# New numbers for the build-time ordering of a fused attention and feed-forward kernel

## The chip, the cores and the metric

The kernel runs on one core of one Trainium2 chip. Its time is the device time of one execution in microseconds; a kernel's time is the median of several runs. Beside it stands one execution taken with the profiler, whose engines, transfers and waits the profile shows. Engines are called TensorE (PE), VectorE (DVE), ScalarE (ACT), GpSimd (POOL) and SyncE (SP); SyncE only issues transfers.

## The reference

Causal attention with a decay bias over 8 batches, 8 heads, 576 positions and a head dimension of 64, then a feed-forward layer with an ELU over the 4608 tokens that result.

```python
scores = (1 / sqrt(D)) * q @ k^T                     # B=8, H=8, S=576, D=64
cum = cumsum(maximum(s, 0.0), axis=-1)
scores = where(causal, -1e9, scores + minimum(-(cum[:, :, :, None] - cum[:, :, None, :]), 0.0))
attn = softmax(scores);  out = attn @ v
x = out.transpose(0, 2, 1, 3).reshape(B * S, H * D)  # 4608 x 512
h = x @ w_in                                         # 512 x 2048
g = where(h > 0, h, exp(minimum(h, 0)) - 1)
return g @ w_out                                     # 2048 x 512
```

## The kernel before, in words

**Attention** goes by batch and by pair of heads. The queries of a batch are cut into blocks: 64 first rows (of both heads of a pair at once) and four blocks of 128. The blocks form pieces: first the lower two blocks of batches 0 to 3, then all four blocks of batches 4 to 7, then the upper two blocks of batches 0 to 3. The lower pieces of batches 0 to 2 are computed with float32 matmuls (the functions with low in their name); all others split each float32 operand into a high and a low float16 part, which VectorE, ScalarE and GpSimd prepare (prepare_pair). For each block TensorE makes the scores (L1065), VectorE adds the mask and keeps the row minimum of the negated scores (L1068), ScalarE takes the exponential and its sum (L1073), VectorE inverts the sum (L1078, L1079), and the scaled result is split into two float16 parts (the high one at L1125, L1127 or L1129, the low one at L1133, or at L1119 and L1120 on GpSimd). SyncE then turns these tiles with transposing transfers (turned_load, L409, tile T), and TensorE weighs the values with them (L1252). The result x goes to memory.

**The feed-forward part** takes 256 tokens at a time, 18 chunks. The first chunk is computed in float32 (native, L1423 and L1477); for it and for the low attention TensorE needs no split operands. For the others x (xh, xl) and the weights (wp) are split in high and low parts and three float16 products are added: first layer at L1427, then the ELU (L1439, L1446 or L1450, L1459, L1463, L1466), second layer at L1484. The weights come as 64-bit numbers (raws), are turned to float32 and split, at L697 to L717, in the first 160 us.

**The order.** All of this is described as operations of a class Plan. An operation has a priority, tiles that it reads and writes, and one or several ways: an engine, a cost in ns, and the instructions. Plan.issue orders them at build time. It keeps a clock of its own for each engine (free) and for the transfers (pipe). For every operation whose inputs are planned, it takes the earliest start: when the engine is free, when the inputs are ready (the end of the step that makes them plus a delay between the two engines, HOPS or HOP), when a buffer is free, and, for steps marked as users of the port that VectorE and GpSimd share (DVE-SB, Pool), not earlier than PORT_LEAD before the end of the last such step. The operation with the earliest start goes next, the lower priority number first where starts are equal; attention has lower numbers than feed-forward matmuls. Among its ways it takes the one with the least start plus cost, each cost multiplied by a bias of its engine: BIAS at first, STEADY_BIAS once the plan's TensorE is past STEADY_T (130 us of the plan). The bias serves the choice alone; the plan's clock takes the cost itself. A transfer takes its cost on SyncE and lands later by LAG, and not sooner than its bytes at RATE (bytes per ns) behind the transfer before. The order so found is fixed on every engine; at run time an engine waits wherever an input of its next instruction is late. SyncE's transfers stand in one queue in this order too.

In the first 60 us of the plan (FILL_T) a filler, a transpose of the identity (L1547), may go on TensorE where nothing else is planned to start within 350 ns (GAP).

The costs are the numbers in the calls of op, and the functions pe4 (a float32 matmul), pe16 (a float16 one), act_c and act_s, dve_p, dve_1, dve_2, pool_1 and pool_2, all of the number of columns n.

Of the kernel before, what the change touches and what calls it, by code (L numbers as in the profile page):

```python
# [34 lines left out]

LAG, RATE = 1800.0, 225.0
W0, WD = 25, 3
# [7 lines left out]
PRIO_LOW = 10  # L45
SP_COST, SP_SHORT, SP_TURN = 460.0, 600.0, 1320.0

# [49 lines left out]
class Plan:  # L97
# [9 lines left out]
    HOPS = {  # L107
        ("PE", "ACT"): 200.0, ("PE", "DVE"): 200.0, ("DVE", "PE"): 255.0, ("ACT", "PE"): 270.0,
        ("Pool", "PE"): 190.0, ("DVE", "ACT"): 130.0, ("DVE", "Pool"): 200.0,
        ("ACT", "DVE"): 140.0, ("ACT", "Pool"): 170.0, ("Pool", "DVE"): 75.0,  # L110
        ("Pool", "ACT"): 100.0, ("DVE", "DVE"): 75.0, ("PE", "PE"): 0.0, ("ACT", "ACT"): 75.0,
        ("Pool", "Pool"): 50.0,
    }
    HOP = 150.0

    BIAS = {"DVE": 1.3, "DVE-SB": 1.3}
    STEADY_BIAS, STEADY_T = {"DVE": 1.6, "DVE-SB": 1.6, "Pool": 1.5}, 130e3

    PORT_LEAD = {"DVE-SB": 240.0, "Pool": 120.0}

# [74 lines left out]
    def issue(self):  # L195
# [19 lines left out]
        while pending:  # L215
# [55 lines left out]
            self.log.append((engine, start, end, o.prio))  # L271
            free[engine] = end
            for b, k in o.new:
# [33 lines left out]
def pe(n):  # L307

    return max(0.4525 * n, 111.0)


def pe4(n):

    return 4 * pe(n)


def pe16(n):

    return n / 2.4 + 2.5

# [33 lines left out]

@with_exitstack
def kernel(
# [50 lines left out]
    def turned_load(prio, units, dst, src, reads, writes):  # L407

        op(prio, [("SP", SP_TURN, lambda: nc.sync.dma_start_transpose(dst(), src()), LAG,  # L409
                   units * P * P * 2)], reads, writes)  # L410

# [56 lines left out]
    def low_keys(tag):  # L468

        k = plan.buf(sb, [P, 2, LOW], F32, f"kl_{tag}", tag="st", bufs=N_ST)  # L470
        return k, [("Pool-M", pool_1(2 * LOW), lambda: pool.memset(k.v[HB:], 0.0))]

# [3 lines left out]
    def decay_sums():  # L476

        own = slice(HB, HB + 1)

        def row(m):  # L480
            return aux.v.rearrange("p m t -> p (m t)")[own, 2 * m * LOW : 2 * (m + 1) * LOW]

        load(-10, lambda: row(0).rearrange("p (h t) -> p h t", h=2), lambda: s[0:1, :2, :LOW],
             [], [(aux, "row")], 2 * LOW * 4)
        load(-9, lambda: aux.v[:NB, 0], lambda: s.rearrange("b h t -> (b h) t"), [], [(aux, 0)], NB * S * 4)
        op(-10, cleared, [], [(k_first, "sums")])

        def first():
            dve.tensor_scalar(row(0), row(0), 0.0, None, ALU.max)
            for h in range(2):  # L490
                sp, lo = (row(m)[:, h * LOW : (h + 1) * LOW] for m in range(2))
                dve.tensor_tensor_scan(lo, sp, sp, 0.0, ALU.add, ALU.max)
                dve.tensor_scalar(k_first.v[own, h], lo, lo[:, S // 2 : S // 2 + 1], 8.0,
                                  ALU.subtract, ALU.mult)
# [8 lines left out]
        for cost, step in (  # L503
            (460.0, lambda: dve.tensor_scalar(sp(), sp(), 0.0, None, ALU.max)),
            (1350.0, lambda: dve.tensor_tensor_scan(lo(), sp(), sp(), 0.0, ALU.add, ALU.max)),
            (590.0, lambda: dve.tensor_scalar(
                sp(), lo(), lo()[:, S // 2 : S // 2 + 1], 8.0, ALU.subtract, ALU.mult)),
        ):
            op(-9, [("DVE-SB", cost, step)], [], [(aux, 0), (aux, 1)])
        load(15, lambda: sums_dram.v, sp, [(aux, 0)], [sums_dram], NB * S * 4, lag=5000.0)  # L510
# [22 lines left out]
    def weigh(o):  # L533

        def rows():
            t = o.v[HB:, Q2].rearrange("p h t -> p (h t)")
            pool.memset(t, 0.0)
            for m in (2, 1, 0):
                pool.affine_select(
                    out=t, in_=t, compare_op=ALU.is_ge, fill=2.0 ** WEIGHT[m], base=-1 - m,  # L540
                    pattern=[[0, t.shape[1]]], channel_multiplier=1,
                )

        op(60, [("Pool-M", 5200.0, rows)], [], [(o, "weights")])
        op(60, [("Pool-M", 800.0, lambda: pool.memset(o.v[HB:, K2], 0.0))], [], [(o, "aux")])
# [27 lines left out]
    def zero_pad(prio, t, i):  # L573
        if pd[i] > pw[i]:
            op(prio, [("Pool-M", 70.0, lambda: pool.memset(t.v[:, pw[i] : pd[i]], 0.0))], [], [(t, "pad")])

# [60 lines left out]
    def scales_of(prio, spans, dst):  # L637
# [11 lines left out]
        def exponents():  # L649
# [6 lines left out]
        used = [(peaks, m) for at, k in spans for m in range(at, at + k)]  # L656
        op(prio, [("DVE-SB", 60.0 + 70 * n, largest)], used, [tops])
        op(prio, [("PE", pe4(P), lambda: pe_.matmul(flat.v[:, :P], tops.v, ident, start=True, stop=True))],
           [tops], [flat])
        op(prio, [("DVE", 600.0, exponents)], [flat], [own])  # L660
        op(prio, [("PE", pe4(P), lambda: pe_.matmul(every.v[:, :n], all_ones.v, own.v[:, :n], start=True, stop=True))],
# [4 lines left out]
    def weight_scales():  # L666

        scales_of(-600, [(A_IN, NF + 1), (A_OUT, NF + 1)], 0)
        op(-600, [("DVE-SB", 100.0, lambda: power(
            scales.v.bitcast(U32)[:, 3:4], scales.v.bitcast(U32)[:, 1:2], 2 * 127))],  # L670
# [92 lines left out]
    def prepare_low(u):  # L763
# [133 lines left out]
    def group_values(u):  # L897
# [8 lines left out]
        for j in range(NP):  # L906
# [35 lines left out]
    def prepare_pair(u, o):  # L942
# [111 lines left out]
    def softmax_block(prio, tag, native, pt, w, mask, mv, reads, operands, inv, view=lambda v: v):  # L1054
# [4 lines left out]
        for i in range(n):  # L1059
            sc = score_bank(f"sc_{tag}_{i}")  # L1060

            def scores(i=i, sc=sc):
# [3 lines left out]

            op(prio, [("PE", pe4(cw) if native else 2 * max(pe16(cw), 100.0), scores)], reads, [sc])
            op(prio, [("DVE", 84 + dve_p(cw), lambda i=i, sc=sc: dve.tensor_tensor_reduce(  # L1068
                pt.v[:, i * cw : (i + 1) * cw], sc.v[:, :cw], mv(i * cw, cw), scale,
                BIG if i == 0 else mn.v[:, 0:1], ALU.add, ALU.min, mn.v[:, i : i + 1]))],  # L1070
               [sc, mask], [(pt, "data"), mn])
        sm, col, last, ns, up = inv
        op(prio, [("ACT", 480 + w / 1.2, lambda: act.activation(  # L1073
            pt.v[:, :w], pt.v[:, :w], AF.Exp, bias=mn.v[:, n - 1 : n], scale=-1.0,
            accum_out=sm.v[:, col : col + 1]))], [mn], [(pt, "data"), (sm, col)])
        if last:
# [3 lines left out]

            op(prio, [("DVE-SB", 350.0, inverse)], [], [sm])

    def normalize(prio, pt, w, sm, col):
        r = slice(col, col + 1)
        op(prio, [
            ("Pool", 160 + 1.04 * w, lambda: pool.tensor_scalar(
                pt.v[:, :w], pt.v[:, :w], sm.v[:, r], 1.0, ALU.mult, ALU.mult)),
            ("DVE-SB", 220 + 0.7 * w, lambda: dve.tensor_scalar(
                pt.v[:, :w], pt.v[:, :w], sm.v[:, r], None, ALU.mult)),
# [4 lines left out]
    def halved(u, i, pt, sm, col):  # L1094
# [27 lines left out]
        for part, size, label in ((whole, k * P, "whole"), (rest, HB, "rest"))[: 1 + (i == u.last)]:  # L1122
            high, low = ((t16, (i, label, m)) for m in range(2))
            op(prio, [
                ("Pool", 160 + 1.04 * size, lambda part=part: pool.tensor_scalar(  # L1125
                    part(0), own(part), sm.v[:, r], 1.0, ALU.mult, ALU.mult)),
                ("DVE-SB", 220 + 0.7 * size, lambda part=part: dve.tensor_scalar(  # L1127
                    part(0), own(part), sm.v[:, r], None, ALU.mult)),
# [227 lines left out]
    def chunk_scales(ch, rows):  # L1356
# [8 lines left out]
        def steps():  # L1365
# [287 lines left out]
```

## Time and profile before

| what | us |
|---|---|
| median of 3 runs (1038.25 to 1038.91) | 1038.66 |
| the profiled execution's own time | 1034.6 |
| its span, first to last instruction | 1032.8 |
| its mean granted TensorE clock | 0.996 of full |

In the profile a matmul's end is modelled, so that a busy TensorE need not be at its peak, and groups of matmuls overlap each other: their busy times do not add up. An idle time stands with the instruction that ended it and with its releaser. L1427 is line 1427 of the kernel before; out<-in are tile names. The stretches that the prediction uses are these: 0 to 75 us, when weights and first inputs are loaded and TensorE also runs fillers; 75 to 150, the float32 chunk, with the weights being split; 150 to 920, attention and feed-forward together; from 920 to the end, feed-forward alone.

### The profile page before, as it was taken

Reading aid. Unit: us, or ns where it says so; the run is one execution under the profiler, and the core shown is the slowest. Engines: PE = TensorE matmul, PEld = TensorE weight load, DVE = VectorE, ACT = ScalarE, POOL = GpSimd, SP = SyncE. Lnnn points to the kernel's source line nnn. Section 1 sums busy time; section 2 is a strip of 40 time slices with the busy share of each in tenths; the row PEclk is TensorE's granted clock in tenths of the full one; section 3 lists DMA queues with packets and bytes.
Section 4 is the critical chain, followed back from the end, with each engine's and each line's share of the span. In section 5 each row is a group of like instructions: output and inputs, shape, how many; then the busy total and the mean of one; then the engine's idle time right before and its main releaser. Section 6 shows DMA issues by size and latency. Waiting matters only on the chain. (4 is left out here: it accounts for less than half of the span.)

```text
span 1032.8 us, 21782 instructions
## 1 busy us (share of the span) xinstructions
PE 1003.1 (97%) x7305; PEld 688.7 (67%) x7305; DVE 845.2 (82%) x2346; ACT 669.0 (65%) x1559; POOL 295.9 (29%) x487
## 2 busy tenths in 40 slices
PE   8889999999999999999999999999999999999998
PEld 6667656676666666666666666676666676666665
DVE  7999998788988988898889999798988898863232
ACT  4898755666667766776776766666675765644343
POOL 6343452242323323241234242222232123100000
PEclk9999999999999999999999999999999999999999
DMA  7997524589979997999989987979998998841000
GB/s 197 276 289 236 150 72 95 124 190 213 222 166 212 207 192 165 198 202 208 196 174 201 232 179 174 229 181 192 215 198 196 227 202 187 182 94 47 1 21 21
DMA packets 296724, 179.83 MB, mean 174 GB/s; under 512 B 209908, under 2 KB 270564, under 8 KB 296612
## 3 DMA queue, kind: packets, MB, share of 16 engines
q1 hardware_dynamic: 296612, 178.45, 75.7%
q8 instruction: 57, 0.93, 0.4%
q14 instruction: 55, 0.45, 0.2%
HBM read 93.08 MB, written 36.81 MB: 126 GB/s over the span
## 5 line engine op out<-in xcount | busy, mean ns | idle before, releaser
L1427 PE MATMUL h<-xh,wp 128*128 128x256 f16 x2176 | 402.7, 273 | 0.7 <-DVE gg L1466 0.7
L1484 PE MATMUL o<-wp,gg 128*128 128x512 f16 x1632 | 392.7, 380 | 0.5 <-DVE gg L1466 0.5
L1427 PEld LDWEIGHTS <-wp 128*128 128x128 f16 x3264 | 317.4, 98 | 69.7 <-issue 2.1
L1427 PE MATMUL h<-xl,wp 128*128 128x256 f16 x1088 | 297.3, 273 | 1.1 <-DVE xl L1403 1.1
L1484 PEld LDWEIGHTS <-gg 128*128 128x128 f16 x1632 | 157.7, 98 | 144.5 <-DVE gg L1466 1.0
L1073 ACT ACTIVATE p<-p,mn 128x192 f32<-128x192 f32 (+1 forms) x232 | 143.7, 620 | 54.9 <-DVE mn L1068 52.9
L1133 DVE SCALAR_TENSOR_TENSOR p<-p,sm,p 128x512 f16<-128x512 f32 (+3 forms) x257 | 162.8, 662 | 4.9 <-POOL p L1125 2.4
L1459 DVE SCALAR_TENSOR_TENSOR h<-g,cs,h 128x512 f32<-128x512 f32 x136 | 102.0, 750 | 60.5 <-ACT g L1446 59.2
L1125 POOL TENSOR_SCALAR p<-p,sm 128x512 f16<-128x512 f32 (+3 forms) x94 | 65.1, 696 | 290.5 <-DVE sm L1079 117.1
L1439 ACT ACTIVATE g<-h,cs 128x512 f32<-128x512 f32 x136 | 92.8, 682 | 78.0 <-PE h L1427 77.2
L1463 ACT ACTIVATE gg<-h 128x512 f16<-128x512 f32 x132 | 78.3, 593 | 83.2 <-DVE h L1459 79.3
L1068 DVE CUSTOM_DVE_ANT_0 p<-sc,maskw 128x192 f32<-128x192 f32 (+1 forms) x232 | 109.5, 481 | 11.9 <-PE sc L1065 8.5
L1065 PE MATMUL sc<-set 128*128 128x288 f16 (+3 forms) x544 | 112.7, 299 | 4.5 <-DVE mn L1068 4.3
L1466 DVE SCALAR_TENSOR_TENSOR gg<-h,gg 128x512 f16<-128x512 f32 x136 | 93.3, 686 | 16.3 <-ACT gg L1463 15.7
L1129 ACT ACTIVATE p<-p,sm 128x512 f16<-128x512 f32 (+3 forms) x139 | 75.1, 557 | 19.0 <-DVE sm L1079 5.5
L1065 PEld LDWEIGHTS <-set 128*128 128x128 f16 x584 | 55.1, 98 | 41.6 <-issue 8.6
L1252 PE MATMUL av<-T,v 128*64 128x256 f16 (+5 forms) x960 | 62.4, 278 | 2.8 <-DMA T<-p 2.8
L1252 PEld LDWEIGHTS <-v 128*64 128x64 f16 x960 | 48.5, 110 | 23.3 <-issue 12.3
L1446 ACT ACTIVATE g<-g 128x512 f32<-128x512 f32 x81 | 50.9, 628 | 1.9
L428 POOL TENSOR_SCALAR v<-va,scales 128x320 f16<-128x320 f32 (+1 forms) x45 | 26.8, 599 | 64.9 <-PE av L1252 58.3
L1073 ACT ACTIVATION_READ_ACCUMULATOR p<-p,mn 128x1 f32 x232 | 43.7, 188 | 0.0
L1068 DVE CUSTOM_DVE_ANT_0 p<-sc,maskw,mn 128x288 f32<-128x288 f32 x64 | 32.9, 514 | 7.1 <-PE sc L1065 5.5
(200 smaller groups left out, 1261.0 us busy)
## 6 DMA issues: line engine op xcount, KB each, us to landing
set<-spread SPq DMA_DIRECT2D x32, 432.0 KB
spread<-parts_None SPq DMA_DIRECT2D x32, 288.0 KB
set<-spread SPq DMA_DIRECT2D x32, 288.0 KB
raws<-in_w_in_dram SPq DMA_DIRECT2D x16, 512.0 KB
raws<-in_w_out_dram SPq DMA_DIRECT2D x16, 512.0 KB
out_dram<-ost SPq DMA_DIRECT2D x32, 256.0 KB
va<-in_vb_dram SPq DMA_DIRECT2D x16, 352.0 KB
xc<-x_dram SPq DMA_DIRECT2D x22, 256.0 KB
```

The source lines that it names most:

```text
L1065: pe_.matmul(view(sc.v[:, :cw]), l, r, start=n == 0, stop=n == len(pairs) - 1)
L1068: op(prio, [("DVE", 84 + dve_p(cw), lambda i=i, sc=sc: dve.tensor_tensor_reduce(pt.v[:, i * cw : (i + 1) * cw], sc.v[:, :cw], mv(i * cw, c ...
L1073: op(prio, [("ACT", 480 + w / 1.2, lambda: act.activation(pt.v[:, :w], pt.v[:, :w], AF.Exp, bias=mn.v[:, n - 1 : n], scale=-1.0, accum_out ...
L1129: ("ACT", 295 + size / 1.2, lambda part=part: act.activation(part(0), own(part), AF.Copy, scale=sm.v[:, r])),
L1133: ("DVE-SB", dve_2(size), lambda part=part: dve.scalar_tensor_tensor(part(1), own(part), sm.v[:, r], part(0), ALU.mult, ALU.subtract)),
L1252: pe_.matmul(av.v[w.h * HB : (w.h + 1) * HB, dst], w.values.v[:, w.h, kb, v], part(w, kb, m), start=kb == 0 and m == 0 and v == 0, stop=kb ...
L1427: pe_.matmul(columns(k), weight_part(f, 0, part)[1]()[:, c * P : (c + 1) * P], xx.v[:, c], start=(c == 0 and m == 0), stop=(c == NCB - 1 a ...
L1439: op(side, [("ACT", act_c(W) + (0 if native else 90), lambda: act.activation(g.v, hp.v, AF.Exp, scale=1.0 if native else by(3)))], [hp] + ...
L1459: op(side, [("DVE", dve_p(W), lambda: dve.scalar_tensor_tensor(hp.v, g.v, by(2 if sign[0] else 1), hp.v, ALU.mult, ALU.max))], [g, cs], [hp])
L1463: ("ACT", act_c(W), lambda: act.activation(gg.v[:, 0], hp.v, AF.Copy, scale=2.0**-DOWN)),
L1466: op(side, [("DVE", dve_p(W), lambda: dve.scalar_tensor_tensor(gg.v[:, 1], hp.v, 2.0**-DOWN, gg.v[:, 0], ALU.mult, ALU.subtract))], [hp, ( ...
L1484: pe_.matmul(acc[i].v, gg.v[:, g, at], weight_part(f, 1, part)[1](), start=(f == 0 and m == 0), stop=(f == NF - 1 and m == 2),)
```

## The change

Only numbers of the plan change, and in one place how an engine's time is reckoned: after a step on VectorE or ScalarE the engine counts as free 95 ns before the step's result is there (OVERLAP), but not earlier than 40 ns after its start. No instruction is added, removed or altered by itself; the order, the engine of a step with several ways, and how many fillers are put in follow from the plan. The delays between engines become smaller: 35 ns where no pair is named (150 before), 205 instead of 255 or 270 towards TensorE; pairs that stood with 75 to 140 ns (such as VectorE to ScalarE) now have the 35. A transfer takes longer to issue and to land. GpSimd costs have a longer fixed part and a smaller one per column. The biases are nearer to 1.

The diff, cut to its core:

```diff
-LAG, RATE = 1800.0, 225.0
+LAG, RATE = 2300.0, 260.0
-SP_COST, SP_SHORT, SP_TURN = 460.0, 600.0, 1320.0
+SP_COST, SP_SHORT, SP_TURN = 590.0, 680.0, 165.0
     HOPS = {
-        ("PE", "ACT"): 200.0, ("PE", "DVE"): 200.0, ("DVE", "PE"): 255.0, ("ACT", "PE"): 270.0,
-        ("Pool", "PE"): 190.0, ("DVE", "ACT"): 130.0, ("DVE", "Pool"): 200.0,
-        ("ACT", "DVE"): 140.0, ("ACT", "Pool"): 170.0, ("Pool", "DVE"): 75.0,
-        ("Pool", "ACT"): 100.0, ("DVE", "DVE"): 75.0, ("PE", "PE"): 0.0, ("ACT", "ACT"): 75.0,
-        ("Pool", "Pool"): 50.0,
+        ("PE", "PE"): 0.0, ("PE", "ACT"): 200.0, ("PE", "DVE"): 200.0,
+        ("DVE", "PE"): 205.0, ("ACT", "PE"): 205.0, ("Pool", "PE"): 205.0,
+        ("DVE", "Pool"): 97.0, ("ACT", "Pool"): 97.0, ("Pool", "Pool"): 90.0,
+        ("DVE", "SP"): 60.0, ("ACT", "SP"): 60.0, ("Pool", "SP"): 60.0,
     }
-    HOP = 150.0
+    HOP = 35.0
+    OVERLAP = {"DVE": 95.0, "ACT": 95.0}
-    BIAS = {"DVE": 1.3, "DVE-SB": 1.3}
-    STEADY_BIAS, STEADY_T = {"DVE": 1.6, "DVE-SB": 1.6, "Pool": 1.5}, 130e3
-    PORT_LEAD = {"DVE-SB": 240.0, "Pool": 120.0}
+    BIAS = {"DVE": 1.15, "DVE-SB": 1.15}
+    STEADY_BIAS, STEADY_T = {"DVE": 1.3, "DVE-SB": 1.3, "Pool": 1.0}, 130e3
+    PORT_LEAD = {"DVE-SB": 400.0, "Pool": 300.0}
...
-            free[engine] = end
+            free[engine] = max(start + 40.0, end - self.OVERLAP.get(engine, 0.0))
...
 def pe4(n):
-    return 4 * pe(n)
+    return 1.667 * n + 12.0
 def pe16(n):
-    return n / 2.4 + 2.5
+    return n / 2.4 + 3.5
 def dve_2(n):
-    return 160 + 1.06 * n
+    return 208 + 1.04 * n
 def pool_1(n):
-    return 120 + 1.04 * n
+    return 255 + 0.87 * n
 def pool_2(n):
-    return 215 + 2.1 * n
+    return 385 + 2.1 * n
...
-        op(prio, [("SP", SP_TURN, lambda: nc.sync.dma_start_transpose(dst(), src()), LAG,
-                   units * P * P * 2)], reads, writes)
+        op(prio, [("SP", max(1350.0, SP_TURN * units), lambda: nc.sync.dma_start_transpose(dst(), src()), LAG,
+                   units * P * P * 2.4)], reads, writes)
...
-            ("Pool", 160 + 1.04 * n,
+            ("Pool", 280 + 0.87 * n,
-            ("DVE-SB", 220 + 0.7 * n, lambda: dve.tensor_scalar(dst(), src(), by(), None, ALU.mult)),
+            ("DVE-SB", 235 + 0.5 * n, lambda: dve.tensor_scalar(dst(), src(), by(), None, ALU.mult)),
...
-        op(-10, [("DVE-SB", 2700.0, first)], [], [(aux, "row"), (k_first, "sums")])
+        op(-10, [("DVE-SB", 4390.0, first)], [], [(aux, "row"), (k_first, "sums")])
-        op(60, [("Pool-M", 5200.0, rows)], [], [(o, "weights")])
+        op(60, [("Pool-M", 8700.0, rows)], [], [(o, "weights")])
...
-        ways = [("DVE-SB", 100 + 1.04 * n, lambda: dve.tensor_reduce(
+        ways = [("DVE-SB", 150 + 1.04 * n, lambda: dve.tensor_reduce(
-            ways.append(("ACT", 480 + n / 1.2, lambda: act.activation(
+            ways.append(("ACT", 290 + n / 1.2, lambda: act.activation(
...
-            op(prio, [("PE", pe4(cw) if native else 2 * max(pe16(cw), 100.0), scores)], reads, [sc])
-            op(prio, [("DVE", 84 + dve_p(cw), lambda i=i, sc=sc: dve.tensor_tensor_reduce(
+            op(prio, [("PE", pe4(cw) if native else 2 * pe16(cw), scores)], reads, [sc])
+            op(prio, [("DVE", 168 + cw + 55 * (i > 0), lambda i=i, sc=sc: dve.tensor_tensor_reduce(
...
-        op(prio, [("ACT", 480 + w / 1.2, lambda: act.activation(
+        op(prio, [("ACT", 383 + w / 1.2, lambda: act.activation(
```

The two lines for scaling on GpSimd and VectorE stand in scaled, normalize and halved alike. Other fixed costs of small steps grow in the same way (exponents 600 to 920, powers 350 to 740, steps 600 to 900, a small memset 70 to 170).

More of the change, by code (lines that the diff above doesn't have):

```diff
@@ L470, in low_keys @@
         k = plan.buf(sb, [P, 2, LOW], F32, f"kl_{tag}", tag="st", bufs=N_ST)
-        return k, [("Pool-M", pool_1(2 * LOW), lambda: pool.memset(k.v[HB:], 0.0))]
+        return k, [("Pool-M", 630.0, lambda: pool.memset(k.v[HB:], 0.0))]
     k_first, cleared = low_keys("first")
@@ L574, in zero_pad @@
         if pd[i] > pw[i]:
-            op(prio, [("Pool-M", 70.0, lambda: pool.memset(t.v[:, pw[i] : pd[i]], 0.0))], [], [(t, "pad")])
+            op(prio, [("Pool-M", 170.0, lambda: pool.memset(t.v[:, pw[i] : pd[i]], 0.0))], [], [(t, "pad")])
     NG = NF // W_GROUP
@@ L656, in scales_of @@
         used = [(peaks, m) for at, k in spans for m in range(at, at + k)]
-        op(prio, [("DVE-SB", 60.0 + 70 * n, largest)], used, [tops])
+        op(prio, [("DVE-SB", 80.0 + 70 * n, largest)], used, [tops])
         op(prio, [("PE", pe4(P), lambda: pe_.matmul(flat.v[:, :P], tops.v, ident, start=True, stop=True))],
            [tops], [flat])
-        op(prio, [("DVE", 600.0, exponents)], [flat], [own])
+        op(prio, [("DVE", 920.0, exponents)], [flat], [own])
         op(prio, [("PE", pe4(P), lambda: pe_.matmul(every.v[:, :n], all_ones.v, own.v[:, :n], start=True, stop=True))],
@@ L668, in weight_scales @@
         scales_of(-600, [(A_IN, NF + 1), (A_OUT, NF + 1)], 0)
-        op(-600, [("DVE-SB", 100.0, lambda: power(
+        op(-600, [("DVE-SB", 150.0, lambda: power(
             scales.v.bitcast(U32)[:, 3:4], scales.v.bitcast(U32)[:, 1:2], 2 * 127))],
@@ L772, in prepare_low @@
         load(prio, lambda: u.q.v[:HB], lambda: qT[b, j, :HB, : 2 * LOW], [], [(u.q, "q")], P * LOW * 4)
-        op(prio if b or j else -10, [("Pool-M", pool_1(2 * LOW), lambda: pool.memset(u.q.v[HB:], 1.0))],
+        op(prio if b or j else -10, [("Pool-M", 630.0, lambda: pool.memset(u.q.v[HB:], 1.0))],
            [], [(u.q, "ones")])
@@ L914, in group_values @@
         scales_of(prio, [(first, NP + 1)], col)
-        op(prio, [("DVE-SB", 100.0, lambda: power(
+        op(prio, [("DVE-SB", 150.0, lambda: power(
             scales.v.bitcast(U32)[:, col + 1 : col + 2], scales.v.bitcast(U32)[:, col : col + 1], 2 * 127 - 15))],
@@ L970, in powers @@
             power(sk2, sq2, 2 * 127)
-        op(prio, [("DVE-SB", 350.0, powers)], [(pk, 0), (pk, 1)], [(pk, 2)])
+        op(prio, [("DVE-SB", 740.0, powers)], [(pk, 0), (pk, 1)], [(pk, 2)])
         def by(m):
@@ L1079, in inverse @@
                 dve.reciprocal(sm.v[:, :ns], sm.v[:, :ns])
-            op(prio, [("DVE-SB", 350.0, inverse)], [], [sm])
+            op(prio, [("DVE-SB", 370.0, inverse)], [], [sm])
     def normalize(prio, pt, w, sm, col):
@@ L1085, in normalize @@
         op(prio, [
-            ("Pool", 160 + 1.04 * w, lambda: pool.tensor_scalar(
+            ("Pool", 280 + 0.87 * w, lambda: pool.tensor_scalar(
                 pt.v[:, :w], pt.v[:, :w], sm.v[:, r], 1.0, ALU.mult, ALU.mult)),
-            ("DVE-SB", 220 + 0.7 * w, lambda: dve.tensor_scalar(
+            ("DVE-SB", 235 + 0.5 * w, lambda: dve.tensor_scalar(
                 pt.v[:, :w], pt.v[:, :w], sm.v[:, r], None, ALU.mult)),
@@ L1124, in halved @@
             op(prio, [
-                ("Pool", 160 + 1.04 * size, lambda part=part: pool.tensor_scalar(
+                ("Pool", 280 + 0.87 * size, lambda part=part: pool.tensor_scalar(
                     part(0), own(part), sm.v[:, r], 1.0, ALU.mult, ALU.mult)),
-                ("DVE-SB", 220 + 0.7 * size, lambda part=part: dve.tensor_scalar(
+                ("DVE-SB", 235 + 0.5 * size, lambda part=part: dve.tensor_scalar(
                     part(0), own(part), sm.v[:, r], None, ALU.mult)),
@@ L1375, in steps @@
             dve.tensor_scalar(cs.v[:, 4:5], cs.v[:, 3:4], scales.v[:, 3:4], 2.0**DOWN, ALU.mult, ALU.mult)
-        op(side, [("DVE-SB", 600.0, steps)],
+        op(side, [("DVE-SB", 900.0, steps)],
            [(scales, 0), (scales, 3)] + [(scales, c) for c in cols if c > 3], [cs])
```

## The prediction

> **What bounds the kernel now.** I read the page's head first, then the busy time of the engines by stretch, the groups of instructions by shape, TensorE's waits, and last the order of time around the largest waits.
>
> ```profile
> span 1032.8 us, 21782 instructions
> ...
> PE 1003.1 (97%) x7305; PEld 688.7 (67%) x7305; DVE 845.2 (82%) x2346; ACT 669.0 (65%) x1559; POOL 295.9 (29%) x487
> ```
>
> ```profile
> core 0: us, PE busy (x) PEld busy (x) DVE busy (x) ACT busy (x) POOL busy (x), PEclk, DMA share, GB/s
> 0.00:75.00 75.00, 64.30 (x418) 48.65 (x420) 64.04 (x202) 55.28 (x170) 35.93 (x87) 0.98 0.90 254
> 75.00:150.00 75.00, 74.11 (x359) 50.73 (x356) 69.94 (x202) 54.75 (x142) 29.59 (x50) 1.00 0.53 163
> 150.00:920.00 770.00, 755.80 (x5772) 516.43 (x5771) 675.62 (x1893) 514.86 (x1178) 230.36 (x351) 1.00 0.87 189
> 920.00:1032.80 112.80, 108.86 (x763) 72.90 (x761) 35.64 (x53) 44.16 (x71) 0.00 (x0) 1.00 0.09 26
> ```
>
> ```profile
> L1547 PE MATMUL scratch<-ident 128*128 128x128 f32 x140 | 19.0, 287 | 0.0
> ```
>
> TensorE (PE) is the bound. Of its 1003.1 us, 19.0 are the fillers of L1547, transposes of the identity that the plan puts where it believes TensorE idle. So 984.1 us are work that no order removes, and 1032.8 - 984.1 = 48.7 us are what an order can touch. By stretch the idle time is 10.7 (0 to 75), 0.9 (75 to 150), 14.2 (150 to 920) and 3.9 us (from 920); the fillers belong to the first. After 920 VectorE's load falls to 35.6 of 112.8 us and GpSimd has nothing: attention is finished and the feed-forward part runs alone. Attention is thus about 110 us ahead of need; delaying it is harmless, making TensorE wait for it is not.
>
> ```profile
> PE sc L1065 <- DVE mn L1068: 5.7, 12, 1.0
> PE sc L1065 <- issue: 3.1, 1, 3.1
> PE av L1252 <- DMA T<-p: 2.8, 3, 1.8
> PE tr_None L1218 <- ACT psh_None L1090: 2.1, 1, 2.1
> PE scratch L1545 <- POOL ident masks.py:199: 2.1, 1, 2.1
> PE tr_None L1218 <- POOL psh_None L1086: 1.5, 2, 0.8
> ```
>
> The columns are total us, number of waits and longest. Nothing repeats every round; these are scattered places in which an operation was put into TensorE's fixed order before its input was there. One of them costs more than its length:
>
> ```profile
> 155.00:157.50 2.50, 2.46 (x11) 1.75 (x12) 2.40 (x12) 2.34 (x5) 1.81 (x3) 0.53 0.62 201
> 157.50:160.00 2.50, 2.50 (x21) 2.10 (x19) 1.58 (x4) 1.38 (x4) 1.92 (x3) 0.79 0.52 139
> ```
>
> The wait of 2.1 us on psh_None ends at 155; behind it the granted clock (the third number from the end) was 0.53 and then 0.79. That loses (0.47 + 0.21) x 2.5 = 1.7 us more, hidden in "busy".
>
> **The change, part by part.** No instruction is added or removed except fillers, whose number follows from the plan. What moves is the order on each engine and the choice of engine where an operation has several ways. So I compare the plan's old and new numbers with rows, then ask which waits they reach.
>
> Start-up durations:
>
> ```profile
> 2.81 1.07 DVE L489 TENSOR_SCALAR aux<-aux 1x640 f32<-1x640 f32 x1 [2.81 <-DMA aux<-in_s_dram]
> ...
> 6.37 0.83 DVE L493 TENSOR_SCALAR kl_first<-aux 1x320 f32<-1x320 f32 x1
> 7.23 0.60 DVE L504 TENSOR_SCALAR aux<-aux 64x576 f32<-64x576 f32 x1
> ```
>
> The first VectorE step runs from 2.81 to 7.20 us, 4.39; the plan had 2700 ns and gets 4390. Everything behind it was planned 1.7 us early.
>
> ScalarE's exponential:
>
> ```profile
> 12.44 0.55 ACT L1073 ACTIVATE p<-p,mn 128x320 f32<-128x320 f32 x1
> 12.89 0.19 ACT L1073 ACTIVATION_READ_ACCUMULATOR p<-p,mn 128x1 f32 x1
> 12.99 0.55 ACT L1073 ACTIVATE pl_both<-pl_both,mn 128x320 f32<-128x320 f32 x1
> ```
>
> Start to start is 0.55 us, the result 0.64. The old plan held the engine for 480 + 320/1.2 = 747 ns; the new gives 383 + 267 = 650 for the result and 95 less, 555, for the engine. Both are right now.
>
> VectorE and GpSimd in attention:
>
> ```profile
> L1133 DVE SCALAR_TENSOR_TENSOR p<-p,sm,p 128x512 f16<-128x512 f32 x128 | 104.4, 841 | 1.6 <-ACT p L1129 1.2
> ...
> L1466 DVE SCALAR_TENSOR_TENSOR gg<-h,gg 128x512 f16<-128x512 f32 x136 | 93.3, 686 | 16.3 <-ACT gg L1463 15.7
> ...
> L1068 DVE CUSTOM_DVE_ANT_0 p<-sc,maskw 128x288 f32<-128x288 f32 x64 | 28.9, 451 | 4.4 <-PE sc L1065 3.4 <-issue 0.5 <-ACT gg L1463 0.3
> ...
> L1125 POOL TENSOR_SCALAR p<-p,sm 128x512 f16<-128x512 f32 x37 | 31.3, 847 | 157.4 <-DVE sm L1079 57.3 <-DMA T<-p 21.9 <-ACT gg L1463 20.6
> ...
> L1127 DVE TENSOR_SCALAR p<-p,sm 128x512 f16<-128x512 f32 x32 | 15.6, 488 | 2.8 <-DMA T<-p 1.9
> ```
>
> Softmax's first step at 288 columns: 539 ns before, 456 now, 451 in the trace. Scaling 512 columns on VectorE: 578, now 491, trace 488. On GpSimd: 692, now 725, trace 847, still short. The remainder at 512 (L1133): 703, now 740, but minus 95 for the engine, against 841: also short.
>
> SyncE's queue:
>
> ```profile
> 299.77 2.85 SPq L409 DMA_TRANSPOSE T<-p  x1
> ```
>
> The widest turned load, 17 units, held the queue 2.85 us; the plan had 1320 ns for every one and gets 165 x 17 = 2805. Every load, store and turn passes this one queue in order, and behind a transpose that runs 1.5 us over stand the next unit's q and k loads, the spreads and the x chunks. The delay from issue to landing also grows from 1800 to 2300 ns in the plan. This is the part that reaches the 2.8 us of "av <- T": with the load planned later, the weighing of L1252 is put behind more feed-forward work, which hides it.
>
> Delays between engines:
>
> ```profile
> 154.39 0.16 DVE L1079 RECIPROCAL sm_None<-sm_None 128x1 f32<-128x1 f32 x1
> ...
> 154.58 0.40 ACT L1090 ACTIVATE psh_None<-psh_None,sm_None 128x128 f32<-128x128 f32 x1 [3.06 <-DVE sm_None L1079]
> ...
> 155.04 0.43 PE L1218 MATMUL tr_None<-ident,psh_None 128*128 128x128 f32 x1 [2.13 <-ACT psh_None L1090]
> ```
>
> VectorE to ScalarE took 154.58 - 154.55 = 0.03 us; the plan had 130 ns and gets 35. ScalarE to TensorE took 155.04 - 154.98 = 0.06; the plan had 270 and gets 205, so some 145 ns of reserve stay at the door that matters.
>
> Choice of engine: from 130 us of the plan on, VectorE's costs are no longer multiplied by 1.6 but 1.3, GpSimd's by 1.0 and not 1.5, ScalarE's by 1 as before. Work leaves ScalarE (514.9 of 770 us busy) for GpSimd (230.4) and, for scaling, VectorE: 491 x 1.3 = 638 is now below ScalarE's 295 + 512/1.2 = 722, where 578 x 1.6 = 925 was above.
>
> **The sum.** Start: idle 10.7 + fillers 19.0. The cover there is not TensorE: DMA engines were busy 0.90 of 75 us and VectorE 64.0, so at most 7.5 us can go; at worst a wrong order adds as much as the largest single hole, some 5. I take a third of the 7.5, -2.5, since only the first step is badly mis-costed by a row. Middle: idle 0.9 + 14.2 plus the 1.7 at half clock, 16.8; nearest rows are the waits. Of "av <- T" I take 2 of 2.8; of the wait at 155 with its slow clock (2.1 + 1.7) half, since the corrected numbers do not contain what made VectorE late there; of the remaining 10.2 a sixth, 1.7, since the softmax numbers now fit. Together -5.6, bounds -16.8 and +15 (the waits doubled). Tail: the last outputs and their eviction, untouched, 0. Sum -8.1: a profiled span of 1024.7, where that execution's own time was 1034.6 (1.8 outside the span). The median of the runs is 1038.66, 4.1 above that execution; the same shift gives 1034.6 - 8.1 + 4.1 = 1030.6, taken as 1031. What is late next is TensorE's own 984.1 us of work, so nothing beyond the 48.7 can follow.
>
> **The rivals.**
>
> 1. *Waits change place, not number* (1037 to 1041). Most waits are single accidents of order; a new order has its own. For it: no wait above repeats. Against it: the numbers moved towards the rows. That the order hardly changes at all is in here too; with nearly every cost altered it is improbable.
>
> 2. *The reserve is gone* (slower, 1046). The old numbers were too long in many places: 150 ns default delay, 747 against 555 ns of ScalarE. Where feed-forward matmuls can always fill in, a plan that expects results too late costs TensorE nothing; a plan that expects them on the dot makes it wait for every disturbance. One softmax chain loses 95 + 105 + 95 ns of planned delay and 97 in the exponential, about 0.4 us, as long as the average "sc <- mn" wait (5.7/12 = 0.48). The price is the 15.1 us of waits after 75 us again: doubled, 1038.7 - 2.5 + 15.1 = 1051; two thirds of that, 1046. It decides where results come later than planned by more than the 145 ns left at TensorE's door. Against it: that rest, the longer landing delay, and the longer GpSimd and SyncE costs.
>
> 3. *GpSimd and VectorE in each other's way* (slower, 1043). In the rows the same operation takes 841 ns with both operands in SBUF (L1133) and 686 with one in PSUM (L1466). At 128 instructions that is 19.8 us, beside 230 us of GpSimd work. If that work grows by half, as 1.5 to 1.0 allows, VectorE gains some 10 us, and its 94 us of idle time in the middle are scattered. With 7 of the 10 reaching TensorE and the start's gain kept: 1038.7 - 2.5 + 7 = 1043. It decides once VectorE's share in the middle, now 88%, passes some 92%. The Trainium skill, page "SBUF — State Buffer", section "Who interferes with whom", says that a VectorE instruction with two SBUF inputs and a GpSimd instruction that reads SBUF exclude each other for the whole instruction. The trace agrees in direction (841 against 686); by that rule the plan's wider allowance (a VectorE step may be placed up to 400 ns before GpSimd ends, 240 before) plans time that is not there, and the sum would come out as this rival's.
>
> **How the numbers follow.** A measurement of this kernel tells about 0.2%, 2 us, from no change. Forecast, fewer losses, 0.58: 1031, by itself 1019 to 1036. Rival 1: 0.15. Rival 2: 0.18. Rival 3: 0.09. So faster 0.58, same 0.15, slower 0.27. The range runs from 1019 (the start's -2.5 and all 16.8 of the middle give 1019.4) to 1046, which takes in rival 3 and the lower half of rival 2; what is left out is about a tenth above and less below.
>
> **What would show it.** Right: TensorE's idle time from 150 to 920 falls from 14.2 towards 9 us, "av <- T" nearly vanishes, the clock row shows no slow stretch near 155, idle plus fillers before 75 us fall below 29.7, ScalarE's busy time falls and GpSimd's rises. Rival 2 shows as more and longer "sc <- mn" and "h <- gg" waits at an unchanged L1133; rival 3 as L1133 above 841 and VectorE above 92% in the middle. The prediction is wrong if the sum of idle and fillers does not fall by some 8 us, or if TensorE's remaining 984.1 us change.

## The result and the profile after

The change made the kernel slower: 1068.48 us median against 1038.79, a ratio of 1.0281 (95% interval 1.0257 to 1.0304). The profiled execution took 1069.99 us, with a span of 1068.2, which is 35.4 more than before. That is more than the 29.7 between the medians, because the profiled execution of before (1034.6) lay 4.2 below its median and this one 1.5 above.

The head of the page, then the busy time by stretch, with the columns as before:

```profile
span 1068.2 us, 21881 instructions
...
PE 1018.8 (95%) x7324; PEld 691.4 (65%) x7324; DVE 865.8 (81%) x2419; ACT 645.0 (60%) x1544; POOL 265.2 (25%) x426
```

```profile
0.00:75.00 75.00, 65.14 (x430) 51.35 (x431) 60.25 (x196) 56.52 (x173) 33.76 (x81) 0.98 0.82 238
75.00:150.00 75.00, 72.48 (x365) 50.16 (x364) 66.86 (x212) 59.42 (x162) 27.11 (x48) 1.00 0.56 168
150.00:920.00 770.00, 736.91 (x5545) 493.31 (x5544) 682.31 (x1926) 487.05 (x1146) 200.30 (x291) 1.00 0.88 190
920.00:1068.20 148.20, 144.24 (x989) 96.53 (x987) 56.36 (x88) 42.01 (x66) 4.07 (x6) 1.00 0.07 22
```

```profile
L1550 PE MATMUL scratch<-ident 128*128 128x128 f32 x159 | 22.1, 292 | 0.0
```

TensorE's idle time went from 10.7 to 9.9 us up to 75, from 0.9 to 2.5 up to 150, from 14.2 to 33.1 up to 920, and stayed at 4.0 behind. That is 19.7 us more. Fillers (L1547 before, L1550 now, since the file is three lines longer) cost 3.1 us more. The remaining 12.6 us stand as busy time: 1018.8 - 22.1 = 996.7 for the same matmuls that took 984.1 before. Most of this can be read as waits too. A first-layer matmul is recorded with 273 ns, while 24 in a row took 2.62 us before, 109 each; so the first 164 ns of a wait behind it pass as busy. The trace has idle time in front of 45 of TensorE's matmuls before the change and of 117 after; 72 more at 164 ns each come to 11.8 us, an estimate that is close to the 12.6. The waits themselves, as total us, number and longest:

```profile
PE sc L1068 <- DVE mn L1071: 18.9, 42, 1.4
PE o L1487 <- DVE gg L1469: 2.8, 4, 1.1
PE sc_None L1068 <- DMA set<-spread: 2.5, 3, 1.4
PE scratch L1548 <- POOL ident masks.py:199: 2.1, 1, 2.1
...
PE av L1255 <- DMA T<-p: 1.4, 2, 0.8
```

The first row carries most of the added idle time, 13.2 of 19.7 us: TensorE stands before a block's scores because VectorE has not yet read the scores that lie in that PSUM bank (L1071, L1068 before). It was 5.7 us in 12 waits. The waits became more, not longer: 0.45 us each against 0.48.

The choice of engine, in the groups by shape:

```profile
L1462 DVE SCALAR_TENSOR_TENSOR h<-g,cs,h 128x512 f32<-128x512 f32 x136 | 102.0, 750 | 6.5 <-ACT g L1449 0.9
L1136 DVE SCALAR_TENSOR_TENSOR p<-p,sm,p 128x512 f16<-128x512 f32 x127 | 97.3, 790 | 1.8 <-ACT p L1132 0.7 <-POOL p L1128 0.6
...
L1453 DVE TENSOR_SCALAR g<-g 128x512 f32<-128x512 f32 x97 | 41.2, 425 | 76.5 <-ACT g L1442 76.1
...
L1130 DVE TENSOR_SCALAR p<-p,sm 128x512 f16<-128x512 f32 x42 | 23.1, 551 | 0.8
```

VectorE took steps from both others: 97 of the ELU's L1453, which were 63 before (L1450), and 42 of the 512-column scalings, which were 32. GpSimd's instructions fell from 487 to 426. The remainder of 512 columns (L1136, before L1133) took 790 ns, less than the 841 before. At 384 columns it took 708 against 657, and the scaling of 512 columns (L1130) 551 against 488. These rows point both ways, so they do not show that VectorE and GpSimd were more in each other's way.

### The profile page after: what moved, and what is told of

Read it like the earlier page. It is cut to its first block, busy times and chain, and to the rows that moved or that the text cites. A ratio compares the mean times of both kernels' runs of the same rounds, so it can differ in the third digit from the quotient of the medians.

```text
span 1068.2 us, 21881 instructions
## 1 busy us (share of the span) xinstructions
PE 1018.8 (95%) x7324; PEld 691.4 (65%) x7324; DVE 865.8 (81%) x2419; ACT 645.0 (60%) x1544; POOL 265.2 (25%) x426
## 5 line engine op out<-in xcount | busy, mean ns | idle before, releaser
L1487 PE MATMUL o<-wp,gg 128*128 128x512 f16 x1632 | 388.0, 379 | 3.1 <-DVE gg L1469 2.8
L1076 ACT ACTIVATE p<-p,mn 128x192 f32<-128x192 f32 (+1 forms) x232 | 143.9, 621 | 74.4 <-DVE mn L1071 68.9
L1136 DVE SCALAR_TENSOR_TENSOR p<-p,sm,p 128x512 f16<-128x512 f32 (+3 forms) x262 | 160.3, 633 | 2.2 <-ACT p L1132 0.7
L1466 ACT ACTIVATE gg<-h 128x512 f16<-128x512 f32 x132 | 78.6, 595 | 132.4 <-DVE h L1462 130.0
L1068 PE MATMUL sc<-set 128*128 128x288 f16 (+3 forms) x544 | 110.3, 297 | 21.5 <-DVE mn L1071 16.8
L1128 POOL TENSOR_SCALAR p<-p,sm 128x512 f16<-128x512 f32 (+3 forms) x86 | 59.6, 697 | 238.4 <-DVE sm L1082 128.0
L1469 DVE SCALAR_TENSOR_TENSOR gg<-h,gg 128x512 f16<-128x512 f32 x136 | 93.2, 685 | 30.9 <-ACT gg L1466 30.4
L1071 DVE CUSTOM_DVE_ANT_0 p<-sc,maskw 128x192 f32<-128x192 f32 (+1 forms) x232 | 108.2, 479 | 7.3 <-PE sc L1068 5.6
L1462 DVE SCALAR_TENSOR_TENSOR h<-g,cs,h 128x512 f32<-128x512 f32 x136 | 102.0, 750 | 6.5 <-ACT g L1449 0.9
L1453 DVE TENSOR_SCALAR g<-g 128x512 f32<-128x512 f32 x97 | 41.2, 425 | 76.5 <-ACT g L1442 76.1
L1068 PEld LDWEIGHTS <-set 128*128 128x128 f16 x584 | 55.0, 98 | 69.0 <-issue 39.3
L1132 ACT ACTIVATE p<-p,sm 128x512 f16<-128x512 f32 (+3 forms) x121 | 64.4, 539 | 17.6 <-ACT p L1076 7.4
L431 POOL TENSOR_SCALAR xh<-xc,cs 128x512 f16<-128x512 f32 x31 | 25.5, 832 | 161.0 <-PE h L1430 161.0
L1255 PEld LDWEIGHTS <-v 128*64 128x64 f16 x960 | 48.7, 111 | 21.7 <-issue 12.1
L1076 ACT ACTIVATION_READ_ACCUMULATOR p<-p,mn 128x1 f32 x232 | 43.6, 188 | 0.0
```

Of the source, the lines that this page charges most:

```text
L1068: pe_.matmul(view(sc.v[:, :cw]), l, r, start=n == 0, stop=n == len(pairs) - 1)
L1071: op(prio, [("DVE", 168 + cw + 55 * (i > 0), lambda i=i, sc=sc: dve.tensor_tensor_reduce(pt.v[:, i * cw : (i + 1) * cw], sc.v[:, :cw], mv( ...
L1076: op(prio, [("ACT", 383 + w / 1.2, lambda: act.activation(pt.v[:, :w], pt.v[:, :w], AF.Exp, bias=mn.v[:, n - 1 : n], scale=-1.0, accum_out ...
L1132: ("ACT", 295 + size / 1.2, lambda part=part: act.activation(part(0), own(part), AF.Copy, scale=sm.v[:, r])),
L1136: ("DVE-SB", dve_2(size), lambda part=part: dve.scalar_tensor_tensor(part(1), own(part), sm.v[:, r], part(0), ALU.mult, ALU.subtract)),
L1255: pe_.matmul(av.v[w.h * HB : (w.h + 1) * HB, dst], w.values.v[:, w.h, kb, v], part(w, kb, m), start=kb == 0 and m == 0 and v == 0, stop=kb ...
```

## The experiments

Three theories were tried. **E**, rate: the new plan holds VectorE and ScalarE for no longer than they need at best, so lateness piles up, and TensorE waits. **D**, hand-over: the shorter delays between engines took away a fixed reserve; this is rival 2 of the prediction. **C**, choice: more steps went to VectorE. A name that begins with a is the new kernel with something undone, b the kernel before with something added, u the new kernel with two things undone, as below. A ratio is against executions of before on the same chip, whose median was between 1037.1 and 1038.8 us; it can differ a little from the quotient of the medians. Where the text speaks of us that came back, it subtracts medians taken on different chips, so a difference below some 2 us says nothing. "Idle" is TensorE's in us, from the busy time by stretch; it belongs to the one profiled execution, which lies up to 5.7 us from the median of its kernel (a_no_overlap 1051.16).

| kernel | median us | ratio to before (95%) | idle 0 to 150 | idle 150 to 920 |
|---|---|---|---|---|
| before | 1038.79 | 1 | 11.6 | 14.2 |
| after | 1068.48 | 1.0281 (1.0257 to 1.0304) | 12.4 | 33.1 |
| a_no_overlap | 1056.86 | 1.0165 (1.0128 to 1.0202) | 11.0 | 20.8 |
| a_old_delays | 1055.49 | 1.0165 (1.0129 to 1.0201) | 11.3 | 25.7 |
| a_old_bias | 1066.25 | 1.0257 (1.0224 to 1.0290) | 11.0 | 29.4 |
| b_overlap | 1076.62 | 1.0368 (1.0343 to 1.0392) | 15.9 | 33.8 |
| a_both_undone (u) | 1033.39 | 0.9963 (0.9939 to 0.9987) | 11.4 | 9.3 |
| a_rate | 1036.58 | 0.9991 (0.9974 to 1.0008) | 10.2 | 17.2 |
| a_door | 1071.74 | 1.0335 (1.0303 to 1.0367) | 13.3 | 38.3 |
| b_noise | 1039.23 | 1.0014 (0.9999 to 1.0029) | 14.6 | 12.0 |
| a_rate_dve | 1047.13 | 1.0086 (1.0056 to 1.0116) | 11.4 | 22.6 |
| a_rate_act | 1075.18 | 1.0372 (1.0336 to 1.0408) | 15.4 | 34.8 |
| a_rate_20 | 1053.06 | 1.0155 (1.0120 to 1.0191) | 16.1 | 17.7 |
| u_rate_05 | 1044.58 | 1.0088 (1.0054 to 1.0123) | 23.7 | 1.3 |
| u_steady_05 | 1063.08 | 1.0244 (1.0226 to 1.0261) | 10.8 | 30.7 |
| u_start_05 | 1054.58 | 1.0160 (1.0137 to 1.0184) | 23.4 | 7.8 |
| a_steady_10 | 1045.41 | 1.0069 (1.0053 to 1.0086) | 12.1 | 20.3 |
| b_steady_05 | 1043.13 | 1.0049 (1.0033 to 1.0065) | 10.8 | 21.3 |
| u_noise | 1040.45 | 1.0023 (1.0011 to 1.0034) | 9.0 | 14.6 |
| u_noise2 | 1037.87 | 1.0001 (0.9985 to 1.0016) | 11.2 | 13.5 |

### Undoing one part, adding one part

a_no_overlap:

```diff
-    OVERLAP = {"DVE": 95.0, "ACT": 95.0}
+    OVERLAP = {}
```

> The new kernel with one thing undone: an engine counts as free only when the step's result is there (OVERLAP empty); all other new numbers stay. Theory E (engine time: the new plan holds VectorE and ScalarE for no longer than the chip needs at best, so a late step is never made up and TensorE waits behind it): most of the 29.7 us comes back, 1038 to 1048, TensorE idle from 150 to 920 below 20 us (33.1 in the new kernel, 14.2 before). Theory D (the shorter delays between engines took the reserve): little comes back, 1060 to 1068. Theory C (the choice of engine): little, 1060 to 1068.

a_old_delays, the whole table HOPS as before, and

```diff
-    HOP = 35.0
+    HOP = 150.0
```

> The new kernel with the old delays between engines (the pairs and the default of 150 ns) and all else new. Theory D: most of the 29.7 us comes back, 1038 to 1048, and the waits of the scores on the row minimum fall from 18.9 us to below 9. Theory E: a delay shifts a result but gives an engine no time to catch up, so at most a third comes back, 1058 to 1068. Theory C: nothing, 1065 to 1070.

a_old_bias:

```diff
-    BIAS = {"DVE": 1.15, "DVE-SB": 1.15}
-    STEADY_BIAS, STEADY_T = {"DVE": 1.3, "DVE-SB": 1.3, "Pool": 1.0}, 130e3
-    PORT_LEAD = {"DVE-SB": 400.0, "Pool": 300.0}
+    BIAS = {"DVE": 1.3, "DVE-SB": 1.3}
+    STEADY_BIAS, STEADY_T = {"DVE": 1.6, "DVE-SB": 1.6, "Pool": 1.5}, 130e3
+    PORT_LEAD = {"DVE-SB": 240.0, "Pool": 120.0}
```

> The new kernel with the old biases and the old allowance at the shared port (BIAS, STEADY_BIAS, PORT_LEAD of before), all else new. Theory C (more steps went to VectorE, which is the fullest of the three): most comes back, 1038 to 1050, and VectorE's instructions fall from 2419 to about 2350. Theories E and D: less than a third comes back, 1058 to 1070.

b_overlap, in the kernel before:

```diff
+    OVERLAP = {"DVE": 95.0, "ACT": 95.0}
-            free[engine] = end
+            free[engine] = max(start + 40.0, end - self.OVERLAP.get(engine, 0.0))
```

> The kernel before with one thing added: VectorE and ScalarE count as free 95 ns before the result (OVERLAP), all else old. Theory E: the old costs were long enough to carry part of it (703 planned, 744 or so traced less 95), so slower, but by less than the full change: 1045 to 1062. Theory D and theory C: 1035 to 1043, since delays and choices are the old ones.

Only a_old_bias came out where E and D had put it; the other three fell between or beyond the bands. OVERLAP and the delays gave back 11.6 and 13.0 us, each some four tenths of the loss, where E and D had each claimed most for its own. The choice gave back 2.2, with overlapping intervals, so C falls as the cause of the loss. With the old biases on the new costs most of GpSimd's steps went to ScalarE (GpSimd busy 115.6 us, ScalarE 733.3), and VectorE's busy time fell from 865.8 to 838.8, without effect on the time. b_overlap missed upwards: OVERLAP alone, on the old costs, cost 37.8 us, more than the whole change. The old costs were not long enough to carry it everywhere: 703 ns planned for the remainder of 512 columns less 95 is 608, against 759 recorded in this kernel.

OVERLAP also moves the choice, since an engine that counts as free sooner is taken sooner. Without it GpSimd was busy 367.8 us with 567 instructions, in the new kernel 265.2 with 426; added to the kernel before it brought GpSimd from 295.9 us down to 172.9. So OVERLAP, and not the new biases, kept work from GpSimd.

### Reserve by rate or at the door

a_both_undone takes both back (no OVERLAP, HOPS and HOP of before); costs, biases and the transfers' numbers stay new. It is called u from here.

> The new kernel with the old delays and without OVERLAP; the new costs, biases, shared-port allowance and transfer numbers stay. Undone singly, the two gave back 11.6 and 13.0 us. If they are two shares of one reserve, they add: 1038 to 1048, TensorE idle from 150 to 920 below 18 us. If the reserve of old costs that were too long (539 ns planned for a softmax step of 451, 747 for 555 of ScalarE) is needed as well: 1048 to 1056.

a_rate leaves delays and OVERLAP new and lengthens the steps on the plan's clock alone, not in the costs that the choice compares:

```diff
+    STRETCH = {"DVE": 1.1, "ACT": 1.1}
-            end = start + cost
+            end = start + cost * self.STRETCH.get(self.ENGINE.get(engine, engine), 1.0)
```

> The new kernel with one thing added: on the plan's clock every step of VectorE and ScalarE takes 1.1 times its cost; delays, OVERLAP, biases and costs for the choice stay new. Theory E (rate: the two engines are booked without any spare time, so lateness piles up): most of the 29.7 us comes back although no delay is longer, 1036 to 1050. Theory D (a fixed reserve at each hand-over is missing): little, 1058 to 1068.

a_door gives the reserve only where TensorE takes over:

```diff
-        ("DVE", "PE"): 205.0, ("ACT", "PE"): 205.0, ("Pool", "PE"): 205.0,
+        ("DVE", "PE"): 705.0, ("ACT", "PE"): 705.0, ("Pool", "PE"): 705.0,
-            return None if was.users else was.until + self.HOP
+            return None if was.users else was.until + self.HOP + 500.0 * (key[1] in ("a", "av"))
```

> The new kernel with 500 ns more planned between any engine and TensorE (705 for 205), and 500 ns more before a score or weighing bank is used again; nothing else. Theory D: the average wait of the scores is 0.45 us, so most go, 1036 to 1050. Theory E: VectorE falls behind the plan by far more than 0.5 us in the course of the kernel, so the waits come back after the first hundred us or two: 1055 to 1068.

b_noise shuffles the order of the kernel before by 2 ns of the default delay:

```diff
-    HOP = 150.0
+    HOP = 152.0
```

> The kernel before with its default delay at 152 ns in place of 150: a change without meaning that shuffles the order a little. Every theory: within 5 us of before, 1034 to 1043; its distance from before tells how much of any difference here can be chance of the order.

The waits of the scores on VectorE in a_both_undone, in a_rate and in a_door:

```profile
PE sc L1069 <- DVE mn L1072: 6.3, 11, 1.2
```

```profile
PE sc L1070 <- DVE mn L1073: 9.8, 13, 1.6
```

```profile
PE sc L1068 <- DVE mn L1071: 21.6, 33, 1.9
```

This decides against D as a reserve at TensorE's door, and shows that E's remedy is enough. With 500 ns of reserve at the door, longer than the average wait of 0.45 us, nothing came back (1071.74, above the bands of both theories, with 21.6 us of such waits and 8.7 more for spread sets). With a tenth more time on the two engines and every delay new, all of it came back (1036.58). By theory E a fixed reserve is used up once and then gone, while an engine booked without spare time does not recover from being late until TensorE's wait lets it. The delays count because a chain of hand-overs with 35 ns each also lets the plan start attention's steps at a faster pace; that reading fits a_old_delays and a_door together, but it is argued: the delays inside a chain and those towards TensorE were not separated otherwise.

Undone together, the two parts give back 35.1 us, more than the sum of 24.6 and more than the whole loss. Two further orders of the same version (the last experiment) give back 28.0 and 30.6, so the excess over the sum is hardly clear of the chance of an order; that the two are shares that add is not excluded. What is sure is that either one left in place is enough to lose. All the other new numbers (costs, biases, transfers) are in this version too, so they do not carry the loss by themselves. b_noise stayed within its band: 2 ns in the delay moved the time by 0.14%.

### Which engine, and how much

a_rate_dve and a_rate_act set STRETCH to {"DVE": 1.1} and to {"ACT": 1.1}; a_rate_20 sets both to 1.2; u_rate_05 sets both to 1.05 in u.

> The new kernel with VectorE's steps alone at 1.1 times their cost on the plan's clock (both engines at 1.1 gave back all of it). VectorE is the fullest engine behind TensorE and the scores wait for it: if its rate alone is the matter, 1036 to 1046. If the fixed reserve per step counts whichever engine has it, about half comes back: 1048 to 1058.

> The new kernel with ScalarE's steps alone at 1.1 times their cost on the plan's clock. If VectorE's rate alone is the matter: 1060 to 1069. If a reserve on either engine slows the planned pace of attention: 1045 to 1058.

> The new kernel with VectorE's and ScalarE's steps at 1.2 times their cost on the plan's clock. If reserve costs TensorE nothing as long as feed-forward matmuls fill in: as 1.1 or a little faster, 1030 to 1038. If too much of it delays attention until the feed-forward part runs out of rows: slower again, 1042 to 1060, with idle time of TensorE on the second layer or on x.

> The version with the old delays and without OVERLAP (0.9963 of before), and VectorE's and ScalarE's steps at 1.05 times their cost on the plan's clock as well. If more reserve still helps: 1026 to 1033. If that version has enough: 1032 to 1038, no difference beyond the chance of the order, some 2 us.

VectorE alone brings 21.4 of the 31.9 us of a_rate, and its 1047.13 lies between the two bands. ScalarE alone brings nothing: 1075.18 is above both of its bands, and slower than the new kernel (1.0372 against 1.0281, intervals apart). A longer clock on ScalarE also sends steps to VectorE, which was busy 881.6 us there against 865.8. VectorE is the engine that must not be booked full; time on ScalarE helps only beside it.

The trace of the new kernel shows how the two engines differ. A step on VectorE or ScalarE is recorded longer than it holds the engine, because the next one may start before the recorded end:

```profile
409.28 0.75 DVE L1462 SCALAR_TENSOR_TENSOR h<-g,cs,h 128x512 f32<-128x512 f32 x1
409.94 0.48 DVE L1071 CUSTOM_DVE_ANT_0 p<-sc,maskw 128x320 f32<-128x320 f32 x1
```

From start to start that is 0.66 us. The table has the means in ns over all steps behind which the next one followed without idle time, beside what the plan holds the engine for, the cost less 95:

| step of the new kernel | recorded | start to start | plan holds |
|---|---|---|---|
| VectorE L1462, ELU, 512 columns | 750 | 660 | 592 |
| VectorE L1136, remainder, 512 | 790 | 712 | 645 |
| VectorE L1469, ELU, 512 | 685 | 602 | 592 |
| ScalarE L1466, 512 | 595 | 499 | 497 |
| ScalarE L1076 with its read, 320 | 649 | 556 | 555 |

ScalarE is booked for as long as it takes, VectorE for less. VectorE's cost of 687 ns for the ELU steps, which the change left alone, was already close to the distance from start to start; OVERLAP took 95 off it again. With the factor 1.1 the plan holds 661 ns for L1462 and 719 for L1136. This fits the outcome of the two runs. It is not the whole loss, for a_no_overlap, which holds 687 and 740, is still 1.65% slower than before.

More reserve was not better. a_rate_20 is 16.5 us slower than a_rate, in the band of its second reading and with the sign named there: TensorE waited 7.0 us for split rows of x (h on xh and xl). u_rate_05 is 11.2 slower than u and above both of its bands, although TensorE hardly idled in its steady stretch. The second and third stretch of u_rate_05:

```profile
75.00:150.00 75.00, 61.62 (x264) 40.78 (x264) 60.07 (x187) 52.81 (x149) 27.62 (x52) 0.84 0.56 167
150.00:920.00 770.00, 768.70 (x5776) 527.59 (x5775) 674.60 (x1855) 500.86 (x1168) 290.92 (x416) 1.00 0.85 185
```

Idle 1.3 of 770 us, but 13.4 from 75 to 150, with the clock granted at 0.84. That asked whether reserve harms at the start alone.

### Reserve at the start or later

The same factor, with a condition: u_steady_05 and u_start_05 are u at 1.05 behind and before 130 us of the plan, a_steady_10 is the new kernel at 1.1 and b_steady_05 the kernel before at 1.05, both behind it.

```diff
+            if free["PE"] > self.STEADY_T:
+                cost *= self.STRETCH.get(self.ENGINE.get(engine, engine), 1.0)
             end = start + cost
```

> The version with the old delays and without OVERLAP, VectorE and ScalarE at 1.05 of their cost on the plan's clock only after 130 us of the plan. With 1.05 from the beginning, TensorE's idle time was 1.3 us from 150 to 920 but 23.7 before 150, against 9.3 and 11.4 without. If the stretches are independent: 11.4 + 1.3 idle and some 1025 to 1031, faster than every kernel so far. If the order behind the start is chance: 1032 to 1040.

> The same version with 1.05 only up to 130 us of the plan. If reserve is harmful at the start, where no feed-forward matmuls can fill in: 1043 to 1055, with the loss before 150 us. If the loss of 1.05 was chance of the order: 1031 to 1040.

> The new kernel, VectorE and ScalarE at 1.1 of their cost on the plan's clock only after 130 us of the plan. If the loss of the change lies in the steady stretch, as the idle time says (33.1 against 14.2 us there, 12.4 against 11.6 before 150): 1034 to 1045. If the start's order is at fault as well: 1048 to 1060.

> The kernel before, VectorE and ScalarE at 1.05 of their cost on the plan's clock only after 130 us of the plan. If the old numbers had less reserve than would serve: 1025 to 1034. If they had enough, or too much: 1036 to 1050.

u_start_05 met its expectation: the idle time of 23.4 us before 150 is that of u_rate_05. a_steady_10 gave back 23.1 of the 29.7 us, its time just above the expected band, so the steady stretch held most of the loss. b_steady_05 came to 1043.13, in the band for old numbers that had enough reserve or too much. u_steady_05 missed the band of independent stretches by more than 30 us, and so did the thought that the stretches are independent. Its 30.7 us of idle time are not many short waits but a few large ones. One of them, from 366 to 382 us, in the busy time and in TensorE's groups by shape:

```profile
366.00:382.00 16.00, 8.13 (x50) 4.71 (x47) 15.01 (x45) 8.75 (x22) 7.28 (x10) 0.68 0.92 234
```

```profile
L1073 PE MATMUL sc<-set 128*128 128x320 f16 (+3 forms) x14 | 4.6, 442 | 5.3 <-DVE mn L1076 5.3
L1435 PE MATMUL h<-xh,wp 128*128 128x256 f16 x10 | 2.7, 339 | 0.0
L1435 PE MATMUL h<-xl,wp 128*128 128x256 f16 x5 | 1.7, 332 | 0.0
```

In 16 us only 15 first-layer matmuls ran, all from 379 us on, and none of the second layer: the feed-forward part had no rows left. Its next rows were split on ScalarE and VectorE only at 377.2 and 378.4 us (xh and xl). TensorE waited for attention, which VectorE, busy 15.0 of 16 us, had to bring up first. The granted clock fell to 0.68 on top. From 150 to 920 VectorE was busy 654.7 us in this kernel and 678.6 in u: booked with too much reserve, it seems to stand idle earlier, where it should get ahead; the two sums alone do not show which came first. In u_rate_05 the late start had put the feed-forward part itself back, so that it did not run dry later; this is argued from the two idle times and not shown by a run of its own.

### Is the lead of u real?

u_noise and u_noise2 are u with a default delay of 152 and 148 ns.

> The version with the old delays and without OVERLAP (0.9963 of before, 0.9939 to 0.9987), with its default delay at 152 ns in place of 150: does its small lead hold when the order is shuffled? If the new costs with a reserve are better: 1030 to 1036. If the lead was chance of the order: anywhere from 1033 to 1045.

> The same with 148 ns in place of 150. If the new costs with a reserve are better: 1030 to 1036. If the lead was chance of the order: anywhere from 1033 to 1045.

It was the chance of one order: 0.9963, 1.0023 and 1.0001 for three orders with the same reserve. The new costs with the old reserve are as fast as before, within some 0.4% either way. No version here beats the kernel before for a reason that the runs show.

## Why the prediction was wrong

It forecast 1031 us and gave slower 0.27; the time lies above its range. Step by step:

- **What bounds the kernel** held: TensorE's own work, plus waits and fillers. The 984.1 us of work stayed the same work; 12.6 us of waits hid in its busy time, which the prediction did not count as something that an order can touch.
- **The numbers beside the rows** were read rightly: most new costs are nearer to the recorded durations. What failed is the step from there to the sum, in the words "of the remaining 10.2 a sixth, 1.7, since the softmax numbers now fit", and with it the middle's -5.6. The middle and the 75 us before it gained 20.5 us of idle time instead, and probably most of the 12.6. The prediction compared a cost with a recorded duration, and looked at the time for the engine, 95 less, only for ScalarE, where it is right (555), and for L1133, where it called 645 short and gave it no term in the sum. On VectorE it is short in every row of the table above: 592 against 660 and 645 against 712 from start to start. Each misses by little, and to the same side, on an engine that was busy 89% of this stretch. The sum treated waits as errors of single numbers; a_rate, which lengthens every step alike and takes the loss back, shows that they go with the pace of all steps together.
- **The start** did not gain 2.5 us: idle time fell by 0.8, fillers rose by 3.1.
- **"av <- T"** was put at -2 of 2.8 us and came to 1.4: right in direction, smaller. The slow clock near 155 went, and another came near 233, behind two waits for spread sets.
- **Choice of engine**: ScalarE's busy time fell, from 514.9 to 487.1 us in the middle, but GpSimd's fell as well, from 230.4 to 200.3. The prediction looked at the biases alone, and those do favour GpSimd (with the old ones and the old allowance at the port it was busy 115.6 us in all, with the new ones 265.2). It left out that OVERLAP makes VectorE and ScalarE free sooner, which takes steps from GpSimd (367.8 us without it).
- **Rival 2** named the mechanism by its outcome: the reserve was gone, and half of its sign, more "sc <- mn" waits at an L1133 that is not longer, is what the profile shows; the longer waits and those of "h <- gg" that it had also named did not come. Its point of decision, 145 ns at TensorE's door, was wrong, as a_door shows, and with it the price of at most 15.1 us: by theory E spare time on VectorE sets a pace for 770 us, where a fixed reserve counts once. The evidence against it, the reserve left at the door, had no weight.
- **"Delaying it is harmless"**, said of attention because it ends 110 us ahead, is wrong where the delay is large: in u_steady_05 the feed-forward part ran out of rows near 366 us, and in a_rate_20 TensorE waited for them.
- **Rival 3** did not occur: L1133 went from 841 to 790 ns and VectorE's share of the middle from 88% to 89%. Rival 1 fits what b_noise and the three orders of u do.

## What to carry to other kernels

In an order fixed at build time, a cost is also a promise; costs, overlaps and delays at their shortest leave the second-fullest engine no way to make up lateness, and the bound engine pays with many short waits. Compare a cost with the distance from start to start before an overlap is taken off it. Put the reserve on the engine that feeds the bound one, as time per step and not as a delay at the last hand-over, and not so much that the work in stock runs out: here 1.1 was right, 1.0 and 1.2 were both slower, each in one order. Before a small gain of a reordering is believed, shuffle the order with a change that means nothing; here that alone moved the time by up to 0.6%.

## What was not expected of the hardware

TensorE's granted clock fell to half for waits shorter than the stretch at half rate that followed, some 3.4 us: the wait of 2.1 us in the kernel before cost 1.7 us more, after waits of 0.8 and 1.4 us in the kernel after the clock was 0.50 from 232.5 to 235 us, and in u_steady_05 waits of 3.2, 1.2 and 2.0 us between 366 and 382 us brought the mean to 0.68. This was rare: in the kernel after, it happened only there between 150 and 920 us, among many short waits. The last first-layer matmul before a wait is recorded some 164 ns longer than its share, so that waits shorter than that do not show as idle time at all.
